# Attention scores in four quadrants, maximum subtracted on GpSimd, transposes and value products two units later

## The chip, the cores and the metric

The kernel runs on one core of a Trainium2 chip. The metric is the device time in microseconds (us) from start to end of one execution. The core has a matrix engine (TensorE, in profiles PE, with its weight loads as PEld), VectorE (DVE), ScalarE (ACT), GpSimd (POOL) and SyncE (SP), which here issues the transfers from main memory (DMA).

## The reference

Three stages follow each other. Sparse attention over 4 batches and 8 heads of 576 positions and head size 64; then a layer that mixes all tokens into 32 slots, passes the slots through eight small expert networks and mixes them back; then a gated feed-forward layer (2304 tokens, 512 to 1536 and back).

```python
scores = scale * np.matmul(q, k.transpose(0, 1, 3, 2))
mask_local = (rel >= 0) & (rel < stride)                  # stride = 32
mask_strided = (rel >= 0) & (pos[None, :] % stride == pos[:, None] % stride)
scores = np.where(masks[None, :, :, :], scores, -1000000000.0)
scores = scores - np.max(scores, axis=-1, keepdims=True)
attn = np.exp(scores)
attn = attn / (np.sum(attn, axis=-1, keepdims=True) + 1e-09)
return np.matmul(attn, v).astype(np.float32)
...
logits = x @ phi
slot_input = d.T @ x                     # d: softmax of logits over tokens
h = np.maximum(slot_input[e] @ w1[e], 0.0); slot_out[e] = h @ w2[e]
return (c @ slot_out)                    # c: softmax of logits over slots
...
return (silu * val @ w_out)              # silu = g * sigmoid(g), g = x @ w_gate, val = x @ w_val
```

## The kernel before

Attention goes in 16 units; a unit is two batches (b = 0, 1) of one head, with queries and keys of batch b on partitions 64b to 64b+63. For the strided heads the positions are permuted, so that every query block of 64 (there are 9, index i) needs a window of 96 keys at most. A unit passes through these steps:

- `qk`: per block and batch one matmul of 64 rows, 64 output partitions and 96 columns, in float32, which takes two instructions each (36 a unit, "sc"). Batch b reads partitions 64b up and writes partitions 64b up. VectorE scales and adds the mask in two pieces of 5 and 4 blocks (480 and 384 columns) and reduces each to the negated maximum `mx`.
- `expo`: nine ScalarE exponentials of 96 columns, with `mx` as bias.
- `tr`: nine transposes by TensorE, and three ScalarE copies into `attile`, one buffer for all units.
- `pv`: 36 instructions of 65 columns (values and a column of ones), then on VectorE the division by the sum into the tile `x`.
- `load_v` brings the next values (64 partitions); GpSimd copies three pieces down to 32 more partitions (L283). Two buffers for values, three for queries and keys.

Every two units, `xtr` (nine transposes of `x`) and `logits` follow; once per pair of batches come `tok_...`, `etr` (transposes of the slot weights) and `slot` (36 instructions, L453). `tok_copy` and `e_perm` are copies of logits and exponentials. The loop over n works on unit n in `qk`/`expo` and on unit n-1 in `tr`/`pv`. All engines run their queues in the order in which the code is written; lists (`at_step`, `at_mid`, `at_first`, `at_late`) put side work into a turn of the loop. Weights of the experts stream in meanwhile: each half tile is 512 KB, `WSCHED` says how many are issued in a turn, from the same SP queue as queries, keys and values. Their homes are 15 buffers of 1 MB and, late, the buffers of attention that come free. `conv` turns packed 64-bit weights into float32 (10 steps a tile, two on ScalarE and eight on VectorE); `PRECONV` and `EXCONV` say how many steps in which turn.

In the feed-forward stage a step n computes gate and value products (`gv`: 2 matmuls, a SiLU on ScalarE, a product on VectorE, a rounded copy `hh` on ScalarE, and the rest `hl` on GpSimd), and three steps later (`LAG`) the output products `omm`; `evac` copies finished sums out of PSUM on VectorE and ScalarE. `room` decides when conversions of later weights are put in.

## Time and profile before

| | us |
|---|---|
| median of three runs (lowest, highest) | 344.02 (342.22, 344.08) |
| the profiled execution | 345.55 |
| its span, first to last instruction | 343.8 |
| TensorE busy in the span | 330.6 |
| VectorE, ScalarE, GpSimd busy | 226.3, 192.8, 121.4 |

The span holds three stretches: attention and slots up to 106.1 us, expert networks up to about 141 us, and feed-forward up to the end. A busy time is an engine's own instructions; the profiled execution has 1.75 us outside its span.

### The profile page before, as it was taken

The numbers are of one execution on the slowest core, as the hardware profiler recorded it, in microseconds if no ns is written. First come the engines' busy times: TensorE is split into PE (matmuls) and PEld (weight loads), VectorE is DVE, ScalarE is ACT, GpSimd is POOL, SyncE is SP. The second block draws the span as 40 slices with busy tenths as digits, with TensorE's granted clock in tenths as the row PEclk, the third lists the DMA queues.
The fourth block names the chain that finished last, engine by engine and source line by source line (L and its number), as shares of the span: only waits on it lengthen the run. The fifth ranks groups of instructions, "written<-read, shape, count | busy, mean of one in ns | idle before, by whom it ended". The sixth has DMA issues, their size and how long they took to land.

```text
span 343.8 us, 7397 instructions
## 1 busy us (share of the span) xinstructions
PE 330.6 (96%) x2857; PEld 248.2 (72%) x2857; DVE 226.3 (66%) x475; ACT 192.8 (56%) x457; POOL 121.4 (35%) x140
## 2 busy tenths in 40 slices
PE   8979999999999999989998999999999999999995
PEld 5868888778775442557785777777878888888894
DVE  6958988998661357477978989899882241424332
ACT  3967899786730123566766576655554343534351
POOL 2133232223200200242353365744577344343441
PEclk9989999999999999998999999999999999999999
DMA  7999999997999999903333544460000030111131
GB/s 277 414 409 375 390 380 378 408 403 248 356 413 400 410 408 408 376 7 124 124 122 126 204 143 139 128 240 1 0 2 0 1 122 3 61 61 62 63 123 61
DMA packets 20803, 71.93 MB, mean 209 GB/s; under 512 B 2336, under 2 KB 2720, under 8 KB 20768
## 3 DMA queue, kind: packets, MB, share of 16 engines
q1 hardware_dynamic: 20624, 71.45, 54.9%
q8 instruction: 22, 0.36, 0.4%
q14 instruction: 13, 0.11, 0.1%
q10 hardware_dynamic: 144, 0.01, 0.0%
HBM read 66.73 MB, written 4.72 MB: 208 GB/s over the span
## 4 chain that ended last, share of the span: by engine, by line
PE 81%; ACT 7%; DVE 5%; DMA 4%; issue 2%; DVEq 0%; SPq 0%; POOL 0%; POOLq 0%
PE o L848 42%; PE pv L742 4%; PE pv L338 4%; PE sc L651 4%; PE sc L305 4%; PE gv L821 4%; PE tr L322 3%; PE gv L822 3%; ACT tmp L315 3%; DMA v<-in_vh 2%; PE tr L357 2%; PE gv L801 2%; DMA k<-in_kq 2%; PE lg L379 1%; PE gv L808 1%
## 5 line engine op out<-in xcount | busy, mean ns | idle before, releaser
L830 POOL TENSOR_TENSOR hl<-h,hh 128x512 fp32r<-128x512 f32 (+1 forms) x60 | 72.5, 1208 | 103.0 <-ACT hh L829 102.9
L848 PE MATMUL o<-woh,hh 128*128 128x512 f32 (+1 forms) x224 | 87.0, 390 | 2.3 <-ACT acc L873 2.2
L848 PE MATMUL o<-wol,hh 128*128 128x512 f32 (+1 forms) x224 | 86.5, 389 | 0.0
L828 DVE TENSOR_TENSOR h<-gv,sg 128x512 f32<-128x512 f32 (+1 forms) x59 | 37.6, 637 | 61.7 <-ACT sg L827 44.1
L848 PE MATMUL o<-woh,hl 128*128 128x512 f32 (+1 forms) x224 | 66.7, 391 | 0.0
L829 ACT CAST hh<-h 128x512 fp32r<-128x512 f32 (+1 forms) x60 | 34.7, 578 | 51.1 <-DVE h L828 51.1
L848 PEld LDWEIGHTS o<-woh,hh 128*128 128x128 f32 x224 | 42.3, 189 | 12.3 <-ACT acc L873 3.0
L848 PEld LDWEIGHTS o<-woh,hl 128*128 128x128 f32 x224 | 42.3, 191 | 9.2
L848 PEld LDWEIGHTS o<-wol,hh 128*128 128x128 f32 x224 | 42.4, 189 | 8.8
L827 ACT ACTIVATE sg<-gv 128x512 f32<-128x512 f32 (+1 forms) x60 | 33.3, 556 | 24.7 <-PE gv L821 22.6
L283 POOL COPY v<-v 32x390 f32<-32x390 f32 (+1 forms) x48 | 22.6, 503 | 63.4 <-DMA v<-in_vh 47.6
L315 ACT ACTIVATE tmp<-tmp,mx 128x96 f32<-128x96 f32 x144 | 40.2, 368 | 8.3 <-DVE mx L310 8.1
L305 PE MATMUL sc<-k 64*64 64x96 f32 x576 | 27.4, 245 | 0.6 <-DMA k<-in_kq 0.5
L305 PEld LDWEIGHTS sc<-k 64*64 64x64 f32 x576 | 24.4, 133 | 3.0 <-issue 1.4
L821 PE MATMUL gv<-cs,St 128*128 128x512 f32 (+1 forms) x60 | 25.6, 426 | 0.0
L338 PEld LDWEIGHTS pv<-v,tmp 96*64 96x64 f32 x576 | 20.0, 140 | 6.3 <-ACT tmp L323 5.7
L792 POOL TENSOR_TENSOR wol<-wo,woh 128x512 fp32r<-128x512 f32 x12 | 15.3, 1301 | 25.5 <-ACT woh L789 25.5
L338 PE MATMUL pv<-v,tmp 96*64 96x65 f32 x576 | 22.3, 229 | 2.0 <-DMA v<-in_vh 1.8
L323 ACT COPY tmp<-tr 96x384 f32<-96x384 f32 x48 | 19.6, 478 | 7.9 <-PE tr L322 7.8
L822 PE MATMUL gv<-cs,St 128*128 128x512 f32 (+1 forms) x59 | 22.3, 378 | 1.1 <-DVE h L828 0.8
L322 PE MATMUL tr<-cst_t,tmp 128*96 128x128 f32 x144 | 21.0, 281 | 1.0 <-ACT eT L443 0.7
L243 DVE SCALAR_TENSOR_TENSOR cv<-g,cv 128x512 int32<-128x512 int32 x30 | 20.8, 692 | 0.7
(165 smaller groups left out, 448.0 us busy)
## 6 DMA issues: line engine op xcount, KB each, us to landing
w<-in_w SPq DMA_DIRECT2D x47, 512.0 KB, 8.5
g<-in_wgv SPq DMA_DIRECT2D x10, 1024.0 KB, 5.0
k<-in_kq SPq DMA_DIRECT2D x16, 576.0 KB, 7.8
g<-in_wo SPq DMA_DIRECT2D x5, 1024.0 KB, 4.9
v<-in_vh SPq DMA_DIRECT2D x16, 292.5 KB, 6.1
wx<-in_w SPq DMA_DIRECT2D x9, 512.0 KB, 6.9
out<-osb SPq DMA_DIRECT2D x17, 256.0 KB, 2.1
w<-in_wgv SPq DMA_DIRECT2D x4, 512.0 KB, 8.8
```

The source lines that it names most:

```text
L283: POOL.tensor_copy(t4[0:W - 64, :, i0:i1, :], t4[64:W, :, i0 - 1:i1 - 1, :])
L305: PE.matmul(out=ps[h, W * (i - i0):W * (i - i0) + W], lhsT=q[h, 64 * i:64 * i + 64], rhs=k[h, c0:c0 + W], start=True, stop=True, skip_grou ...
L315: ACT.activation(out=e[:, i], in_=e[:, i], func=AF.Exp, scale=1.0, bias=mx[:, i:i + 1])
L322: PE.transpose(ps[0:W, 128 * j:128 * j + 128], e[:, 3 * t + j], ident)
L338: PE.matmul(out=ps[64 * b:64 * b + 64, 65 * (i - i0):65 * (i - i0) + 65], lhsT=attile[0:W, i, 64 * b:64 * b + 64], rhs=v[0:W, 65 * (NT * b ...
L821: PE.matmul(out=pg[:, 0:n], lhsT=St[f][:, 0:128], rhs=csf[:, t0:t0 + n], start=True, stop=True)
L822: PE.matmul(out=pvv[:, 0:n], lhsT=St[f][:, 128:256], rhs=csf[:, t0:t0 + n], start=True, stop=True)
L827: ACT.activation(out=sg[:, 0:n], in_=pg[:, 0:n], func=AF.Silu)
L828: DVE.tensor_tensor(out=h[:, 0:n], in0=pvv[:, 0:n], in1=sg[:, 0:n], op=ALU.mult)
L829: ACT.copy(hh[bi, f][:, 0:n], h[:, 0:n])
L830: POOL.tensor_tensor(out=hl[bi, f][:, 0:n], in0=h[:, 0:n], in1=hh[bi, f][:, 0:n].bitcast(F32), op=ALU.subtract)
L848: PE.matmul(out=o[:, 0:c], lhsT=(a, a, l)[i][:, 128 * t:128 * t + 128], rhs=(woh, wol, woh)[i][f][:, c * k:c * k + c], start=(first and i ...
```

## The change

Each unit's 18 score products are spread over all four quadrants of the array: batch b still reads row half b, but even and odd blocks write output halves 0 and 1, and each batch has a PSUM bank of its own. `place(b, i)` says in which slot of the score tile, and on which half of its partitions, a block then stands. A 19th product fills the part of the last slot that a full-width read covers. VectorE adds the masks in three pieces (480 and 384 columns, and 96 on half the partitions). GpSimd adds the negated maximum to the scores, in two pieces; `expo` is two exponentials without bias. `expo` works on unit n-1, `tr` and `pv` on unit n-2, and `tr` is the first thing of a turn. The strided masks are five tiles instead of nine. Copies of `xtr` are all on ScalarE, so are `tok_copy`, and `e_perm` of the first pair. `WSCHED` and `TL` set the turns of weight loads anew, `PRECONV`, `EXCONV`, `ORDER` and `ROOMS` those of conversions. In the feed-forward stage the `hh` and `hl` of the first two steps (`DEFER`) are written one step later.

```diff
-EXCONV = {12: 2, 13: 2, 14: 2, 19: 1, 20: 1, 21: 1, 22: 1}
+EXCONV = {12: 2, 13: 3, 14: 1, 17: 1, 19: 1, 20: 1, 21: 1}
...
-MSC = 6
+MSC = 2
+DEFER = 2
...
+TOKA = (0, 1)
+TOKB = (0,)
...
-XTD = {(1,1,1):(0,1),(1,0,0):(0,1,2)}
+XTD = {}
...
-ROOMS = (0.8, 1.2, 0.6)
+ROOMS = (0.8, 1.2, 0.3)
...
-WSCHED = [2]*12+[2,2,2,2,0]
+WSCHED = [1, 0, 3, 2, 3, 2, 2, 2, 1, 2, 2, 1, 3, 2, 3, 3, 2, 2, 4]
...
+def place(b, i):
+    return (2 * (i // 2) + b, i % 2) if i + 1 < NT else (i, b)
...
-        for i0, i1 in zip(CUT, CUT[1:]):
-            ps = bank("sc", 2)
-            for i in range(i0, i1):
-                c0 = 64 * i
-                for b in range(2):
-                    h = slice(64 * b, 64 * b + 64)
-                    PE.matmul(out=ps[h, W * (i - i0):W * (i - i0) + W], lhsT=q[h, 64 * i:64 * i + 64],
-                              rhs=k[h, c0:c0 + W], start=True, stop=True, skip_group_check=True)
...
+        bk = [bank("sc", 2) for _ in range(2)]
+        last = NT - 1
+        for i, b, c in [(2 * g + d, b, d) for g in range(4) for b, d in ((0, 0), (1, 1), (0, 1), (1, 0))] + \
+                [(last, 0, 0), (last, 1, 1), (last, 0, 1)]:
+            h = slice(64 * b, 64 * b + 64)
+            PE.matmul(out=bk[b][64 * c:64 * c + 64, W * (i // 2):W * (i // 2) + W], lhsT=q[h, 64 * i:64 * i + 64],
+                      rhs=k[h, 64 * i:64 * i + W], start=True, stop=True, skip_group_check=True)
...
+        for o, p, m in ((e[:, 0:9:2], p5[0], m5), (e[:, 1:8:2], p5[1][:, 0:4], m5[:, 0:4]),
+                        (e[64:128, last], p5[1][64:128, 4], m5[64:128, 4])):
+            DVE.scalar_tensor_tensor(out=o, in0=p, scalar=0.125, in1=m, op0=ALU.mult, op1=ALU.add)
+        for s0, s1 in zip(CUT, CUT[1:]):
+            DVE.tensor_reduce(out=mx[:, s0:s1], in_=e[:, s0:s1], axis=AX, op=ALU.max, negate=True)
+            POOL.tensor_tensor(out=e[:, s0:s1], in0=e[:, s0:s1],
+                               in1=mx[:, s0:s1].unsqueeze(2).to_broadcast([128, s1 - s0, W]), op=ALU.add)
...
-        for i in range(CUT[k], CUT[k + 1]):
-            ACT.activation(out=e[:, i], in_=e[:, i], func=AF.Exp, scale=1.0, bias=mx[:, i:i + 1])
+        a = etile(u)[:, CUT[k]:CUT[k + 1]]
+        ACT.activation(out=a, in_=a, func=AF.Exp)
...
-        while n < 16 or any(k >= n for k in late):
...
+        while n < 18 or any(k >= n for k in late):
+            if 2 <= n < 18:
+                tr(n - 2)
             if n < 16:
                 qk(n)
                 load_qk(n + NQK)
             if 0 <= n - 1 < 16:
-                tr(n - 1)
...
+                expo(n - 1, 0)
...
+            if 2 <= n < 18:
+                pv(n - 2)
+                load_v(n)
...
             ACT.activation(out=sg[:, 0:w], in_=pg[:, 0:w], func=AF.Silu)
+            while late_hh:
+                late_hh.pop(0)()
...
+            if n < DEFER:
+                late_hh.append(split)
+            else:
+                split()
```

Two turns of TensorE's queue in the middle of attention, before ("sc" are the scores, "tr" over `tmp` the transposes of a unit, "tr" over `x` those of `xtr`, "lg" the logits, `k_76` to `k_78` the three buffers of queries and keys, `v_79` and `v_80` those of values):

```order
L305 MATMUL sc<-k_76 64x96 x18
L322 MATMUL tr<-cst_t,tmp 96x128 x9
L379 MATMUL lg<-xT,phi_t 32x16x18 x4
L338 MATMUL pv<-v_80,tmp 64x65 x18
L305 MATMUL sc<-k_77 64x96 x18
L322 MATMUL tr<-cst_t,tmp 96x128 x9
L338 MATMUL pv<-v_79,tmp 64x65 x18
L357 MATMUL tr<-cst_t,x 128x128 x9
```

The same place of TensorE's queue after the change, also two turns:

```order
L337 MATMUL tr<-cst_t,tmp 96x128 x9
L316 MATMUL sc<-k_77 64x96 x19
L395 MATMUL lg<-xT,phi_t 32x16x18 x4
L354 MATMUL pv<-v_80,tmp 64x65 x18
L337 MATMUL tr<-cst_t,tmp 96x128 x9
L316 MATMUL sc<-k_78 64x96 x19
L354 MATMUL pv<-v_79,tmp 64x65 x18
L373 MATMUL tr<-cst_t,x 128x128 x9
```

The transposes moved ahead of the scores, so that the scores now stand between every `tr` and its `pv`.

GpSimd's queue at the start of the loop, before (`v0` and `v1` are the two buffers of values, each copied in three pieces):

```order
L283 COPY v0_79<-v0_79 32x2x130
L283 COPY v0_79<-v0_79 32x2x195 x2
L283 COPY v1_80<-v1_80 32x2x130
L283 COPY v1_80<-v1_80 32x2x195 x2
L283 COPY v0_79<-v0_79 32x2x130
```

The same stretch of GpSimd's queue after the change (`mx_134`, `mx_167`, `mx_225`, `mx_306` are the maxima of units 0 to 3):

```order
L295 COPY v0_79<-v0_79 32x2x130
L295 COPY v0_79<-v0_79 32x2x195 x2
L295 COPY v1_80<-v1_80 32x2x130
L295 COPY v1_80<-v1_80 32x2x195 x2
L325 TENSOR_TENSOR tmp_83<-tmp_83,mx_134 128x480
L325 TENSOR_TENSOR tmp_83<-tmp_83,mx_134 128x384
...
L325 TENSOR_TENSOR tmp_83<-tmp_83,mx_225 128x480
L325 TENSOR_TENSOR tmp_83<-tmp_83,mx_225 128x384
L295 COPY v0_79<-v0_79 32x2x130
L295 COPY v0_79<-v0_79 32x2x195 x2
L325 TENSOR_TENSOR tmp_83<-tmp_83,mx_306 128x480
```

The additions of a unit now stand behind the value copies of the unit before it.

ScalarE's queue at the start of the feed-forward stage, before (`sg` is the SiLU, `hh` the rounded copy, `wg` a conversion step, `acc` an evacuation):

```order
L827 ACTIVATE sg<-gv 128x512
L829 CAST hh<-h 128x512
L827 ACTIVATE sg<-gv 128x512
L829 CAST hh<-h 128x512
L221 ACTIVATE wg_2157<-g 128x512 x2
L827 ACTIVATE sg<-gv 128x512
L829 CAST hh<-h 128x512
```

The same place of ScalarE's queue after the change:

```order
L838 ACTIVATE sg<-gv 128x512 x2
L844 CAST hh<-h 128x512
L233 ACTIVATE wg_2106<-g 128x512 x2
L838 ACTIVATE sg<-gv 128x512
L844 CAST hh<-h 128x512 x2
```

The first two copies `hh` moved one step down, behind the next step's SiLU.

## Rows read from the trace of the kernel before

**Rows 1.** The page: busy us (share of the span) xinstructions of three engines

```profile
PE 330.6 (96%) x2857; PEld 248.2 (72%) x2857; DVE 226.3 (66%) x475; ACT 192.8 (56%) x457; POOL 121.4 (35%) x140
```

**Rows 2.** Windows: span; PE, PEld, DVE, ACT, POOL busy; clock; DMA share, GB/s

```profile
20.00:30.00 10.00, 9.87 (x162) 8.34 (x160) 5.49 (x16) 6.08 (x20) 3.28 (x9) 0.83 1.02 409
40.00:50.00 10.00, 10.00 (x185) 8.46 (x183) 8.33 (x22) 9.03 (x30) 3.19 (x7) 1.00 1.01 386
50.00:60.00 10.00, 10.00 (x189) 8.63 (x187) 8.56 (x23) 9.08 (x29) 3.21 (x8) 1.00 1.01 382
150.00:160.00 10.00, 8.34 (x28) 6.14 (x28) 6.66 (x11) 5.95 (x11) 3.32 (x4) 0.83 0.33 107
```

**Rows 3.** The chain that ended last, two units: start us, us, what

```profile
39.10 1.77 PE sc L305 x36
40.87 1.12 PE tr L322 x9
...
43.33 1.13 PE tr L357 x9
...
47.25 0.62 PE lg L379 x8
47.88 1.20 PE pv L338 x36
49.08 1.63 PE sc L305 x36
```

**Rows 4.** The same chain, landmarks of attention

```profile
11.26 8.40 DMA v<-in_vh
...
22.26 2.08 PE tr L357 x9
...
75.04 2.15 PE tr L453 x36
...
91.53 2.36 PE tr L357 x18
...
106.10 13.44 PE sc L651 x119
```

**Rows 5.** Groups by line and shape: busy us, mean ns, idle before

```profile
L315 ACT ACTIVATE tmp<-tmp,mx 128x96 f32<-128x96 f32 x144 | 40.2, 368 | 8.3 <-DVE mx L310 8.1
L309 DVE SCALAR_TENSOR_TENSOR tmp<-sc,mt 128x480 f32<-128x480 f32 x16 | 10.4, 651 | 1.6 <-PE sc L305 1.1 <-ACT wg L221 0.3
L309 DVE SCALAR_TENSOR_TENSOR tmp<-sc,mt 128x384 f32<-128x384 f32 x16 | 8.8, 548 | 0.0
L698 ACT ACTIVATE cf<-cf 96x384 f32<-96x384 f32 x2 | 1.0, 522 | 2.5 <-DVE cf L696 2.5
L830 POOL TENSOR_TENSOR hl<-h,hh 128x512 fp32r<-128x512 f32 x26 | 33.7, 1296 | 52.3 <-ACT hh L829 52.3
L830 POOL TENSOR_TENSOR hl<-h,hh 128x256 fp32r<-128x256 f32 x4 | 3.0, 738 | 3.9 <-ACT hh L829 3.9
L438 PE MATMUL tr<-cst_t,e 128*64 128x128 f32 x16 | 1.8, 298 | 0.0
L434 PE MATMUL tr<-cst_t,e 128*128 128x128 f32 x16 | 2.4, 283 | 0.0
```

**Rows 6.** Timeline: value copies on GpSimd, a conversion on VectorE; issues of values

```profile
59.61 1.30 POOL L283 COPY v<-v 32x260 f32<-32x260 f32 x3 [3.26 <-DMA v<-in_vh]
72.65 2.23 POOL L283 COPY v<-v 32x260 f32<-32x260 f32 x3 [7.04 <-DMA v<-in_vh]
72.69 1.82 DVE L243 SCALAR_TENSOR_TENSOR wg<-w,wg 128x512 int32<-128x512 int32 x2
v<-in_vh SPq DMA_DIRECT2D x16, 292.5 KB, 6.1
```

**Rows 7.** Start of feed-forward: timeline of TensorE's wait, then the chain

```profile
152.85 0.50 PE L848 MATMUL o<-woh,hh 128*128 128x512 f32 x1 [1.42 <-ACT acc L873]
152.85 4.61 PE o L848 x12
157.92 2.75 PE o L848 x12
```

More of the change, by code (lines that the diff above doesn't have):

```diff
@@ L99, in constants @@
     c[:, 3], c[:, 4], c[:, 5], c[:, 15] = q, q + 32, q + 16, np.maximum(q, 31)
-    for i in range(NT):
-        c[:, 6 + i] = (64 * i + q) // 18 * 18 - 64 * i + 32
+    for g in range(5):
+        i = np.minimum(2 * g + p // 64, NT - 1)
+        c[:, 6 + g] = (64 * i + q) // 18 * 18 - 64 * i + 32
     return c
@@ L337, in pv @@
                 for b in range(2):
-                    PE.matmul(out=ps[64 * b:64 * b + 64, 65 * (i - i0):65 * (i - i0) + 65], lhsT=attile[0:W, i, 64 * b:64 * b + 64],
+                    s, c = place(b, i)
+                    PE.matmul(out=ps[64 * b:64 * b + 64, 65 * (i - i0):65 * (i - i0) + 65], lhsT=attile[0:W, s, 64 * c:64 * c + 64],
                               rhs=v[0:W, 65 * (NT * b + i):65 * (NT * b + i) + 65], start=True, stop=True, skip_group_check=True)
@@ L405, in e_perm @@
         for hf in hfs:
-            DVE.tensor_copy(e2[bp][64:128, 288 * hf:288 * hf + 288].rearrange("p (r t) -> p r t", t=18),
+            (ACT.copy if bp in TOKB else DVE.tensor_copy)(e2[bp][64:128, 288 * hf:288 * hf + 288].rearrange("p (r t) -> p r t", t=18),
                             e2[bp][0:64].rearrange("p (t r) -> p r t", r=32)[:, 16 * hf:16 * hf + 16])
@@ L417, in tok_copy @@
         for hf in range(2):
-            DVE.tensor_copy(Lb[r].rearrange("p (t r) -> p t r", r=32)[:, :, 16 * hf:16 * hf + 16],
+            (ACT.copy if bp in TOKA else DVE.tensor_copy)(Lb[r].rearrange("p (t r) -> p t r", r=32)[:, :, 16 * hf:16 * hf + 16],
                             lg[bp][64 * hf:64 * hf + 64, 0:288].rearrange("p (t r) -> p t r", r=16))
@@ L440, in etr @@
         p4 = ps[:, 0:128 * (z - a)].rearrange("p (j y b s) -> p j y b s", y=2, b=2, s=32)
-        for b, cp_ in ((0, ACT.copy), (1, ACT.copy)):
+        for b, cp_ in ((0, ACT.copy), (1, DVE.tensor_copy if (bp, g) in ETD else ACT.copy)):
             w0, w1 = (max(a, 1), z) if b == 0 else (a, min(z, NT))
@@ L815, in build, with gv @@
         csf = cs.rearrange("p a b -> p (a b)")
-        def gv(bi, f):
-            t0, n = BLOCKS[bi]
+        late_hh = []
+        def gv(n, bi, f):
+            t0, w = BLOCKS[bi]
             n0 = start.pop(0) if start else 2
             pg, pvv = [bank("gv", 3) if k < n0 else bank("o", 4) for k in range(2)]
-            PE.matmul(out=pg[:, 0:n], lhsT=St[f][:, 0:128], rhs=csf[:, t0:t0 + n], start=True, stop=True)
-            PE.matmul(out=pvv[:, 0:n], lhsT=St[f][:, 128:256], rhs=csf[:, t0:t0 + n], start=True, stop=True)
+            PE.matmul(out=pg[:, 0:w], lhsT=St[f][:, 0:128], rhs=csf[:, t0:t0 + w], start=True, stop=True)
+            PE.matmul(out=pvv[:, 0:w], lhsT=St[f][:, 128:256], rhs=csf[:, t0:t0 + w], start=True, stop=True)
             sg = fl.tile([128, 512], F32, tag="sg", name="sg", bufs=2)
@@ L826, in gv, with split @@
             hl[bi, f] = fl.tile([128, 512], F32R, tag="hl", name="hl", bufs=LAG + 1)
-            ACT.activation(out=sg[:, 0:n], in_=pg[:, 0:n], func=AF.Silu)
-            DVE.tensor_tensor(out=h[:, 0:n], in0=pvv[:, 0:n], in1=sg[:, 0:n], op=ALU.mult)
-            ACT.copy(hh[bi, f][:, 0:n], h[:, 0:n])
-            POOL.tensor_tensor(out=hl[bi, f][:, 0:n], in0=h[:, 0:n], in1=hh[bi, f][:, 0:n].bitcast(F32),
-                               op=ALU.subtract)
+            ACT.activation(out=sg[:, 0:w], in_=pg[:, 0:w], func=AF.Silu)
+            while late_hh:
+                late_hh.pop(0)()
+            DVE.tensor_tensor(out=h[:, 0:w], in0=pvv[:, 0:w], in1=sg[:, 0:w], op=ALU.mult)
+            def split(a=hh[bi, f], b=hl[bi, f]):
+                ACT.copy(a[:, 0:w], h[:, 0:w])
+                POOL.tensor_tensor(out=b[:, 0:w], in0=h[:, 0:w], in1=a[:, 0:w].bitcast(F32), op=ALU.subtract)
+            if n < DEFER:
+                late_hh.append(split)
+            else:
+                split()
         ob = {}
@@ L996, in build @@
                 room -= part(n)
-            if n >= STG:
+            m = n + 1 - LAG
+            if n >= STG and not (n in NOSTG or (AVOID and 0 <= m < len(seq) and seq[m][2] == CUTS[seq[m][1]][seq[m][0] + 1] - 1)):
                 stage(n)
```

65 lines of the change are left out of this document (27 added, 38 removed).

## Prediction

> **What bounds the kernel now.** I read the page first: TensorE is busy for 96% of the span [rows 1], so time is won only where TensorE gets less to do or where its work is stretched. The windows say where to look: from 40 to 60 us TensorE is busy all the time, while VectorE (8.3 to 8.6 us of 10), ScalarE (9.0 to 9.1) and DMA (share 1.01, 382 to 386 GB/s) are nearly full too [rows 2]. The chain of waits is a plain TensorE chain there: two units take 49.08 - 39.10 = 9.98 us, 4.99 a unit, made of scores 1.63, transposes 1.12, value products 1.20, and every second unit 1.13 for the transposes of x and 0.62 for logits [rows 3]. The landmarks bound the stretch that the change touches: the value products of unit 2 end at 22.26, those of unit 15 at 91.53, and the experts' weights begin at 106.10, 14.57 us later [rows 4]. So 13 units take 69.3 us. TensorE's own work in them is 13 x (1.63 + 1.12 + 1.20) + 6 x (1.13 + 0.62) + slot transposes (1.8 + 2.4)/2 = 2.1 [rows 5] + slot sums 2.15 [rows 4] = 66.1 us; the other 3.2 are waits and a stretch from 20 to 30 us with a granted clock of 0.83 [rows 2], that is, part of it at 1.2 instead of 2.4 GHz, after TensorE had waited for values (the 8.40 us from the issue of a transfer to its landing, [rows 4]).
>
> **The scores.** 36 instructions take 1.63 us, 45 ns each, on two quadrants [rows 3]. There will be 38 on four. Bounds: no faster, 38 x 45 ns = 1.72 us; twice as fast, 38 x 22.6 = 0.86. The nearest row is the value product, 33 ns an instruction with 65 columns [rows 3], so 0.51 ns a column against the scores' 0.47: neither shows a floor, both go with columns. I take 28 ns, 1.05 us, in the middle between the 33 of that row and 22.6. That takes 0.58 us off each unit's path.
> Beside this, the Trainium skill (TensorE: Matmul & The Clock Gate, in the section Wait — 56ns, not 53.3ns?) says that the distance from one matmul's start to the next does not go below about 25 ns however few columns it has. By that the scores would take 38 x 25 ns = 0.95 us, an estimate from that page, and TensorE's floor below would be 80.5 instead of the 81.6 of my 1.05 us; a full doubling to 0.86 would be out of reach. The densest small product shown here, 33 ns, does not contradict it.
>
> **ScalarE** gives nine exponentials (40.2 us for 144, 0.28 each, 2.5 a unit [rows 5]) for two of 480 and 384 columns. The exponential of 96x384 takes 0.52 [rows 5], so about 0.52 + 0.60 = 1.1. It takes over copies of 0.5 each, one to two a unit at most. ScalarE falls from 9 us of 10 to about 7 and hides.
>
> **VectorE** gets a third mask piece of 96 columns: by 0.651 for 480 and 0.548 for 384 [rows 5], 0.24 us; the moved copies take about as much off. It stays at (8.33 + 8.56)/2 per 10 us x 0.499 = 4.2 us a unit.
>
> **GpSimd** gets two additions. Its subtractions of 128x512 and 128x256 take 1.296 and 0.738 [rows 5], so 480 columns take 1.23 and 384 take 1.02. With 1.30 for the value copies [rows 6] that is 3.55 us a unit, under any of the turns below. They are queued behind the copies, which wait for a transfer: who waits for the addition is the exponential, and for that the transposes. The loop to check is: value products of unit n-2 end, values n land 6.1 us after their issue [rows 6], copies 1.30, additions of n+1 1.23 + 1.02, second exponential 0.52, the last transposes 0.4, scores 1.05, logits 0.3 on average, value products n+1 1.20: 13.1 us in three turns, 4.37 a unit.
>
> **Where attention then ends.** At the start the first additions stand behind both first value copies, which delays unit 0, while fewer weights are ahead of the third values. I let the value products of unit 2 end at 24, 1.7 us later than before (22 to 26). From there four floors hold to the end of unit 15:
> TensorE, with two score sets already done: 24 + 11 x 1.05 + 13 x (1.12 + 1.20) + 7 x 1.13 + 6 x 0.62 + 2.1 + 2.15 = 81.6.
> DMA: before the last values the queue holds 16 x 0.59 MB of queries and keys, 16 x 0.30 of values and, by the new table, 32 half tiles of 0.524: 31.1 MB. At the 409 GB/s of rows 2 this is 76 us, from 1.2 on, then copies 1.3 and product 1.2: 79.7, and up to 2 us later if the queue runs dry in the first turns.
> VectorE: 24 + 13 x 4.2 = 78.6, without pauses.
> The loop over GpSimd: 24 + 13 x 4.37 = 80.8.
> They lie within 3 us, so each one's jitter becomes another's wait. Before, with TensorE's floor well above the rest, 3.2 us were lost; I take 4.1 above the highest floor, 85.7. The gain is 91.53 - 85.7 = 5.8 us. It costs nothing behind it: the 14.57 us up to the experts hold the same steps, and the last weights hang on buffers that attention frees, so they move with it.
>
> **The feed-forward start.** TensorE waits 1.42 us for ScalarE's evacuation, which stands behind a rounded copy that waits for VectorE; then the clock falls, and twelve products take 4.61 us where the next twelve take 2.75 [rows 7], in the window with a granted clock of 0.83 [rows 2]. With the copies moved one step down, ScalarE runs the second SiLU while VectorE makes the first product, and the third copy is done earlier. At most 1.42 + 1.86 = 3.3 us are won, at least none, since conversions on VectorE bind again soon after. I take half, 1.6. The new places of conversion steps and the order of loads I cost at nothing: they are as many as before and lie beside TensorE work.
>
> **The sum** against the profiled execution: 345.55 - 5.8 - 1.6 = 338.1. That execution is 1.53 above the median 344.02, so the time is **336.6**.
>
> **Rivals.**
> First, GpSimd becomes the bound, and the kernel gets slower. Evidence for: three value copies took 2.23 us instead of 1.30 just while VectorE ran two conversion steps for 1.82 us [rows 6], 1.72 times as long; additions are GpSimd work that reads the same memory. If all of GpSimd's 3.55 us were stretched so, a unit would take 6.1 us: 13 x 6.1 = 79.3 instead of 69.3, and with the feed-forward gain 344.0 + 10 + 1.7 - 1.6 = 354. It decides from a stretch of 1.41 on (3.55 x 1.41 = 4.99). Against: only some 16 conversion steps fall into 16 units.
> The Trainium skill (SBUF — State Buffer, in the section SBUF: two separate sides) says that VectorE and GpSimd share a port pair that one locks for a whole instruction, for VectorE steps with two inputs there or in a two-port mode. The pair of rows 6 agrees with that. By it the masks and maxima, which read scores from PSUM or have one input, would not collide, and this rival would not come.
> Second, values come late. If the landing takes 8 us instead of 6.1 because the queue is always full, the loop over GpSimd takes 15 us, 5.0 a unit, as now, and only the waits at the start and in the middle go: attention gains 2, feed-forward 1, 341.
> Third, four quadrants are no faster than two: 1.72 for the scores makes TensorE's floor 81.6 + 11 x 0.67 = 89.0, attention ends at about 90, gain 1.5, and with 1 of feed-forward 341.5.
> Fourth, everything goes well: TensorE's floor is reached (gain 9.9) and the clock does not fall (3.3): 344.0 - 13.2 = 331.
>
> **Chances.** The forecast (334 to 340) 0.50, the fourth 0.15, the second 0.17, the third 0.08, the first 0.08, others 0.02. The range leaves out the first rival and the outermost ends of the fourth and second: 331 to 343. One per cent, 3.4 us, is about what a measurement of this kernel can tell from no change. Faster by more (below 340.6): the forecast, the fourth and half of second and third, 0.78; within it 0.14; slower 0.08.
>
> **What would show it.** The score group should fall from 1.63 us to 0.9 to 1.25; at 1.6 the third rival holds. The exponentials should take 1.1 us a unit, the additions 2.25; at 3.5 or more with TensorE's waits ending in GpSimd, the first. The value products of unit 15 should end at 83 to 88, the first expert product start 14 to 15 us later. If the transposes wait for exponentials, these for additions, and these for value copies that wait for DMA, it is the second. In feed-forward the wait for the evacuation should be shorter and the granted clock in that stretch nearer 1.00. What would make me wrong most easily is the friction of 4.1 us, which no row prices, and the start, where a long idle time of TensorE could lower its clock.

## The result, and the profile after

The changed kernel takes 345.24 us (343.36 to 346.93, nine runs) where the kernel before, run beside it, takes 342.74 (342.22 to 344.08, nine runs): ratio 1.006 [1.0031, 1.0088]. A second comparison on another chip gives 344.69 against 344.13, 1.0004 [0.9976, 1.0033]. One run of again_after and one of quad below were in a slower state of the chip; every ratio goes by the other runs and is not the quotient of the medians beside it. So the change is worth nothing, or costs up to 0.9%; 336.6 was forecast, and the range ended at 343.

The page, busy time by engine. TensorE is busy 10.9 us less than before [rows 1], GpSimd 28 more:

```profile
PE 319.7 (94%) x2889; PEld 237.5 (70%) x2889; DVE 227.2 (67%) x477; ACT 176.1 (52%) x356; POOL 149.6 (44%) x172
```

The windows [rows 2], with the one from 30 to 40 us added. TensorE is not full any more in three of the four windows of attention (in the other its clock is 0.87); the transfers (last two columns: share and GB/s) and VectorE (third busy time) are, in three of four. The granted clock of 0.83 that stood in the feed-forward stage is not seen here:

```profile
20.00:30.00 10.00, 8.95 (x198) 7.23 (x196) 9.68 (x25) 5.49 (x13) 5.88 (x10) 1.00 1.00 386
30.00:40.00 10.00, 6.90 (x120) 5.60 (x116) 9.74 (x20) 4.50 (x11) 5.65 (x9) 0.96 1.02 410
40.00:50.00 10.00, 10.00 (x188) 8.15 (x186) 7.98 (x21) 7.38 (x17) 7.56 (x13) 0.87 0.91 322
50.00:60.00 10.00, 8.79 (x186) 6.91 (x184) 9.57 (x27) 5.90 (x15) 5.93 (x10) 1.00 1.00 369
150.00:160.00 10.00, 10.00 (x50) 7.55 (x49) 8.88 (x15) 7.72 (x16) 5.57 (x5) 1.00 0.30 103
```

The chain that ended last, two units in the middle [rows 3]. The scores are 0.98 us instead of 1.63, but a chain of TensorE alone holds only for a stretch:

```profile
47.92 1.13 PE tr L373 x9
49.06 1.21 PE tr L337 x9
50.27 0.98 PE sc L316 x38
51.25 0.62 PE lg L395 x8
...
60.16 1.01 PE sc L316 x38
61.27 1.14 DVE tmp L322 x2
62.71 1.11 DVE mx L324 x2
64.38 0.82 DVE x L361 x2
66.55 1.04 DVE wg L251 x2
```

From 61 to 82 us it runs through VectorE: masks, maxima, divisions and conversion steps of several units in a row. The start of the same chain [rows 4]: value transfer, both value copies, addition, exponential, and only then the first transposes, which take 2.16 us at half clock where 1.12 is usual.

```profile
1.63 5.04 DMA v<-in_vh
6.73 1.30 POOL v L295 x3
...
8.93 1.31 POOL v L295 x3
10.32 1.00 POOL tmp L325
11.34 0.61 ACT tmp L330
11.99 2.16 PE tr L337 x9
```

The groups that answer to [rows 5] (busy us, mean ns, idle before). Exponentials and the third mask piece are as priced, additions cheaper:

```profile
L330 ACT ACTIVATE tmp<-tmp 128x480 f32<-128x480 f32 x16 | 9.7, 607 | 21.3 <-POOL tmp L325 21.2
L330 ACT ACTIVATE tmp<-tmp 128x384 f32<-128x384 f32 x16 | 8.4, 523 | 3.6 <-POOL tmp L325 3.5
L325 POOL TENSOR_TENSOR tmp<-tmp,mx 128x480 f32<-128x480 f32 x16 | 16.1, 1007 | 5.9 <-PE tr L337 4.3 <-DVE mx L324 0.4 <-ACT xT L375 0.2
L325 POOL TENSOR_TENSOR tmp<-tmp,mx 128x384 f32<-128x384 f32 x16 | 14.7, 916 | 0.0
L322 DVE SCALAR_TENSOR_TENSOR tmp<-sc,mt 64x96 f32<-64x96 f32 x16 | 4.2, 261 | 0.5
L259 DVE SCALAR_TENSOR_TENSOR wg<-w,wg 128x512 int32<-128x512 int32 x4 | 3.9, 987 | 0.0
L237 DVE TENSOR_SCALAR wg<-wg 128x512 f32<-128x512 f32 x4 | 3.6, 938 | 0.0
```

The chain at the start of the feed-forward stage [rows 7]. The second dozen of output products follows the first without a wait or a fall of the clock:

```profile
149.10 3.03 PE o L867 x12
...
152.60 2.75 PE o L867 x12
```

**The landmarks** tell where the time went. I read four from each profile: the end of the value products of unit 2, the time from there to those of unit 15, the first expert product, and the time from the end of the last second-layer expert product to the end of the 37th instruction of the output products ("ff start"). All times in us; ratio and interval are to the kernel before run beside it (its medians there lie between 342.74 and 344.13), so compare ratios and not medians across rows.

| kernel | unit 2 ends | 2 to 15 | experts at | ff start | median time | ratio, interval |
|---|---|---|---|---|---|---|
| before | 22.3 | 69.3 | 106.0 | 22.1 | 342.74 | 1 |
| again_before | 21.2 | 68.9 | 104.6 | 20.5 | 342.82 | one run |
| changed | 24.7 | 68.5 | 107.7 | 18.4 | 345.24 | 1.006 [1.0031, 1.0088] |
| again_after | 25.6 | 68.0 | 108.2 | 18.4 | 344.69 | 1.0004 [0.9976, 1.0033] |
| no_add | 26.1 | 65.1 | 105.7 | 18.4 | 344.21 | 1.0023 [0.9992, 1.0053] |
| no_conv | 24.9 | 69.2 | 108.7 | 18.3 | 344.73 | 1.0008 [0.9975, 1.004] |
| late_copy | 27.8 | 68.6 | 110.9 | 18.3 | 346.54 | 1.0079 [1.0064, 1.0094] |
| nv3 | 28.2 | 65.0 | 107.8 | 19.3 | 347.03 | 1.0091 [1.0066, 1.0116] |
| act_bias | 27.6 | 69.3 | 111.4 | 18.3 | 346.31 | 1.0068 [1.0039, 1.0098] |
| ff_only | 21.1 | 68.9 | 104.5 | 18.3 | 340.6 | 0.9912 [0.9888, 0.9937] |
| quad | 21.2 | 69.5 | 105.2 | 18.5 | 343.35 | 0.9996 [0.9961, 1.0032] |
| lag2 | 28.0 | 68.0 | 110.6 | 18.4 | 348.41 | 1.0133 [1.0084, 1.0181] |
| light | 25.5 | 65.2 | 105.3 | 18.5 | 356.62 | 1.0392 [1.0348, 1.0436] |
| lean | 28.2 | 61.2 | 103.9 | 18.4 | 354.21 | 1.0313 [1.0281, 1.0345] |
| early_w | 25.7 | 69.7 | 110.0 | 18.3 | 343.97 | 1.0021 [0.9998, 1.0044] |
| early_both | 24.6 | 67.1 | 106.3 | 18.4 | 343.45 | 1.0007 [0.9983, 1.0031] |
| quad_w | 21.5 | 73.7 | 109.7 | 18.6 | 344.94 | 1.0067 [1.0036, 1.0097] |
| ff_only_w | 21.6 | 68.7 | 104.9 | 18.3 | 340.88 | 0.9914 [0.9885, 0.9943] |
| early_warm | 26.0 | 65.2 | 105.7 | 18.3 | 343.21 | 0.9987 [0.9966, 1.0007] |

The changed kernel wins 2.1 us at the feed-forward start (3.7 against the first profile of before, where the clock fell there). It loses 3 us in attention, all at the start: unit 2 ends 3.5 us later than in again_before, the second profile of the kernel before. And from unit 2 to unit 15, where 12 sets of scores of 1.63 us are now 11 of 0.98, 8.8 us less for TensorE, it wins less than one. TensorE's work did shrink. Here are 65 us of attention (columns as in the windows) of again_before, then of the changed kernel:

```profile
25.00:90.00 65.00, 63.24 (x1119) 52.35 (x1118) 53.86 (x136) 53.22 (x170) 20.05 (x39) 1.00 0.97 373
```

```profile
25.00:90.00 65.00, 56.87 (x1116) 45.73 (x1115) 58.08 (x147) 41.55 (x95) 39.60 (x62) 0.97 0.96 358
```

TensorE's idle time rose from 1.8 to 8.1 us. So two questions: what fills the 8 us, and what delays the start.

### The profile page after: what moved, and what is told of

It reads as the page before. It is cut to its first block, busy times and chain, and to the rows that moved or that the text cites. A ratio compares the mean times of both kernels' runs of the same rounds, so it can differ in the third digit from the quotient of the medians.

```text
span 341.6 us, 7400 instructions
## 1 busy us (share of the span) xinstructions
PE 319.7 (94%) x2889; PEld 237.5 (70%) x2889; DVE 227.2 (67%) x477; ACT 176.1 (52%) x356; POOL 149.6 (44%) x172
## 4 chain that ended last, share of the span: by engine, by line
PE 78%; DVE 12%; issue 3%; ACT 2%; POOL 2%; DMA 1%; SPq 0%; DVEq 0%; POOLq 0%; ACTq 0%
PE o L867 42%; PE pv L751 4%; PE sc L660 4%; PE gv L832 4%; PE gv L833 3%; PE tr L337 3%; DVE tmp L322 3%; PE sc L316 3%; PE pv L354 3%; DVE mx L324 2%; PE gv L810 2%; DMA v<-in_vh 1%; DVE x L361 1%; PE tr L373 1%; PE gv L817 1%
## 5 line engine op out<-in xcount | busy, mean ns | idle before, releaser
L867 PE MATMUL o<-woh,hl 128*128 128x512 f32 (+1 forms) x224 | 65.9, 387 | 0.0
L867 PEld LDWEIGHTS o<-woh,hl 128*128 128x128 f32 x224 | 41.7, 188 | 9.0
L295 POOL COPY v<-v 32x390 f32<-32x390 f32 (+1 forms) x48 | 20.8, 465 | 32.9 <-DMA v<-in_vh 16.6
L325 POOL TENSOR_TENSOR tmp<-tmp,mx 128x480 f32<-128x480 f32 (+1 forms) x32 | 30.1, 962 | 5.9 <-PE tr L337 4.3
L330 ACT ACTIVATE tmp<-tmp 128x480 f32<-128x480 f32 (+1 forms) x32 | 17.8, 565 | 24.9 <-POOL tmp L325 24.7
L337 PE MATMUL tr<-cst_t,tmp 128*96 128x128 f32 x144 | 21.6, 297 | 7.0 <-ACT tmp L330 3.5
L322 DVE SCALAR_TENSOR_TENSOR tmp<-sc,mt 128x480 f32<-128x480 f32 (+2 forms) x48 | 22.0, 485 | 6.8 <-PE sc L316 4.7
L801 POOL TENSOR_TENSOR wol<-wo,woh 128x512 fp32r<-128x512 f32 x12 | 15.3, 1297 | 25.5 <-ACT woh L798 25.5
L832 PE MATMUL gv<-cs,St 128*128 128x512 f32 (+1 forms) x60 | 25.6, 426 | 0.0
L354 PEld LDWEIGHTS pv<-v,tmp 96*64 96x64 f32 x576 | 18.7, 137 | 8.1 <-issue 3.5
L354 PE MATMUL pv<-v,tmp 96*64 96x65 f32 x576 | 20.7, 224 | 2.8 <-issue 1.2
L337 PEld LDWEIGHTS tr<-cst_t,tmp 128*96 128x96 f32 x144 | 15.7, 133 | 10.5 <-ACT xT L375 4.5
```

The costliest lines, as they stand in the source:

```text
L295: POOL.tensor_copy(t4[0:W - 64, :, i0:i1, :], t4[64:W, :, i0 - 1:i1 - 1, :])
L322: DVE.scalar_tensor_tensor(out=o, in0=p, scalar=0.125, in1=m, op0=ALU.mult, op1=ALU.add)
L325: POOL.tensor_tensor(out=e[:, s0:s1], in0=e[:, s0:s1], in1=mx[:, s0:s1].unsqueeze(2).to_broadcast([128, s1 - s0, W]), op=ALU.add)
L337: PE.transpose(ps[0:W, 128 * j:128 * j + 128], e[:, 3 * t + j], ident)
L354: PE.matmul(out=ps[64 * b:64 * b + 64, 65 * (i - i0):65 * (i - i0) + 65], lhsT=attile[0:W, s, 64 * c:64 * c + 64], rhs=v[0:W, 65 * (NT * b ...
L832: PE.matmul(out=pg[:, 0:w], lhsT=St[f][:, 0:128], rhs=csf[:, t0:t0 + w], start=True, stop=True)
```

## The experiments

Each expectation names its theories, and their letters change from batch to batch. In the first, A is that VectorE is full and the additions stretch its work, B that the additions are a link in the loop from values to value products; in the second, A is the queue on GpSimd, B the two value buffers and C the bytes of all transfers.

**Both kernels again, and one load at a time.** again_before and again_after are the kernels unchanged.

> The kernel before, unchanged, for a second profile. Its first profiled execution took 345.55 us, above all nine timed runs (342.22 to 344.08). If the clock that fell at 153 us there (twelve products in 4.61 us instead of 2.75) is a chance of that execution, this profile shows 2.75 to 3 there and a span of 340 to 342; if it belongs to the kernel, 4.6 again and 343 to 344.

> The changed kernel, unchanged, for a second profile and more timed runs. Both theories (VectorE full and stretched, or the loop over values and additions) expect the value products of unit 15 to end at 92 to 95 us again, and 1.003 to 1.009 of the time before.

The second profile of before shows no fall of the clock anywhere in its span; the 4.61 us of [rows 7] were a chance of that execution. Against it the feed-forward gain is 2.1 us. again_after ends unit 15 at 93.6 us, as expected, but its ratio of 1.0004 lies under the 1.003 to 1.009 expected.

no_add leaves the additions out; no_conv leaves out VectorE's steps of the conversions that run during attention:

```diff
-            POOL.tensor_tensor(out=e[:, s0:s1], in0=e[:, s0:s1],
-                               in1=mx[:, s0:s1].unsqueeze(2).to_broadcast([128, s1 - s0, W]), op=ALU.add)
...
             _, fn, k = q.pop(0)
-            fn(k)
+            if fn.__name__ == "mag":
+                fn(k)
```

> The changed kernel without the two GpSimd additions of a unit: the maximum is still reduced but not subtracted (left out). Theory A, VectorE is the full engine in attention and GpSimd's additions stretch its conversion steps: the steps of conversion go back from about 0.95 us to 0.7, units are no longer held, value products of unit 15 end at 85 to 88, 5 to 7 us off the time. Theory B, the additions matter as a link of the loop (values land, copies, additions, exponentials): the same gain or more, 6 to 9 us, with conversion steps as long as before. If neither holds, under 2 us.

> The changed kernel without VectorE's steps of the 30 early conversion steps (of the first three packed weight tiles only the first ScalarE step is left; what they hold is not the weight). Theory A: VectorE loses 16 steps of about 0.95 us in attention, so units of 20 to 80 us shorten and the value products of unit 15 end 6 to 9 us earlier, at 84 to 87. Theory B: the additions and landings are untouched, at most 2 us.

no_add missed both theories: without additions the units shorten by 3 us, but unit 2 ends later still, at 26.1. no_conv misses A and fits B (at most 2 us), against which no_add speaks: nothing shortens, although VectorE's busy time in the 65 us falls from 58.1 to 46.5. Neither load alone is the bound.

**The value path.** late_copy moves the value copies of a unit behind the next unit's additions; nv3 has a third value buffer, earlier transfers, and copies behind the unit's own additions; act_bias subtracts the maximum as before. (`shift_v` holds the three copies, split off `load_v`.)

```diff
 # late_copy
             if 0 <= n - 1 < 16:
+                shift_v(n - 1)
                 expo(n - 1, 0)
 # nv3
-NB = 15
-NV = 2
+NB = 14
+NV = 3
...
+                shift_v(n)
...
-                load_v(n)
+            if 1 <= n < 15:
+                load_v(n + 1)
 # act_bias: no POOL.tensor_tensor, and in expo
+        for i in range(CUT[k], CUT[k + 1]):
+            ACT.activation(out=e[:, i], in_=e[:, i], func=AF.Exp, scale=1.0, bias=mx[:, i:i + 1])
```

> The changed kernel, except that GpSimd's three value copies of a unit stand one unit later in its queue, behind the next unit's additions instead of ahead of them, so no addition waits for a transfer of values. Theory A (the gain is lost because the additions, and with them the exponentials and TensorE, queue on GpSimd behind copies that wait 5 to 6 us for a transfer): the second and third unit start without the wait of 3.5 us at 12 us, value products of unit 2 end at 21 to 22.5 (24.7 and 25.6 in the two profiles of the changed kernel), units 2 to 15 take 65 to 66 us (68.0 and 68.5), and the time is 5 to 6 us less than the changed kernel's: 338 to 340, ratio to before 0.982 to 0.990. Theory B (the two value buffers: the next transfer starts only when the value products of two units before have ended, lands 5.5 us later and is copied in 1.3): the start gains its 2 to 3 us, units 2 to 15 still take 68, 341 to 342. Theory C (the bytes of all transfers up to unit 15 set its end): the start's gain is given back, unit 15 ends at 93, 343 to 345.

> The changed kernel with three value buffers instead of two and one expert-weight buffer less (two halves of a weight are loaded later for it), the transfer of a unit's values issued one unit earlier, and the value copies behind the unit's own additions. Theory B (two value buffers): values have landed before their copies are due, GpSimd waits for a values' transfer less than 5 us in all up to unit 15 (20 to 30 us before), units 2 to 15 take 62 to 65 us, unit 15 ends at 84 to 88, and the time is 335 to 339. Theory A (queue on GpSimd alone): the same as with the copies moved alone, within 1 us. Theory C (bytes): unit 15 ends at 92 to 94, 343 to 345.

> The changed kernel, with the maximum subtracted as before by nine exponentials of a unit on ScalarE (its bias), and no additions on GpSimd. Theory A (queue on GpSimd): units 2 to 15 take 65 to 67 us, the exponentials' 2.5 us of ScalarE for a unit find room beside 4.5 of a unit, value products of unit 2 end at 22 to 24, and the time is 340 to 342, ratio 0.988 to 0.995. Theories B and C (two value buffers, or bytes): units 2 to 15 take 68 to 69 us as with the additions, 343 to 345.

No theory held for late_copy: it is slower, and GpSimd now waits 18.8 us for maxima and TensorE 5.5 us for value copies. With nv3 the waits for values are gone (GpSimd has none of 0.9 us or more in sum from 15 to 92 us) and the units take 65.0, as B says, but unit 2 ends at 28.2, and the experts, one weight buffer short, take 3 us longer. act_bias brings the old 69.3 back. In all three the start got worse, whatever became of the additions.

**The parts by themselves.** ff_only is the kernel before with `DEFER`, `ROOMS` and the order of the weights 8 and 10; quad adds the four quadrants to it (the matmuls, `place` and the masks of the section on the change) and nothing else: units one step apart, nine exponentials, old tables; lag2 is the changed kernel with the old scores and exponentials: distance and tables alone.

```diff
 # ff_only, quad
-ROOMS = (0.8, 1.2, 0.6)
+ROOMS = (0.8, 1.2, 0.3)
+DEFER = 2
 # lag2, in act_bias
-    return (2 * (i // 2) + b, i % 2) if i + 1 < NT else (i, b)
+    return i, b
...
+        for i0, i1 in zip(CUT, CUT[1:]):
+            ps = bank("sc", 2)
```

> The kernel before with nothing but the three changes at the feed-forward start (two of gate and value kept back, the order of the weights 8 and 10, the third limit 0.3). All theories: attention stays as before, unit 15 ends at 90 to 92 and the experts start at 104.5 to 106; from the end of the second expert products to the end of the 24th output product it takes 18.4 us, where the kernel before took 20.5 in the profile without a fall of TensorE's clock there. So the time is 1.8 to 2.4 us under the kernel before beside it, ratio 0.993 to 0.995. If it is as slow as before, the gain at the feed-forward start hangs on the changed attention.

> The kernel before with the feed-forward start changed and the scores in quadrants (with the masks and places of blocks that go with them), and nothing else: transposes and value products one unit later as before, nine exponentials with the maximum as bias, no additions on GpSimd, all tables as before. Theory S (the quadrants are worth what was expected; the loss comes from the two units' distance, which leaves TensorE empty at the start): value products of unit 2 end at 20 to 22 as before, units 2 to 15 take 61 to 65 us instead of 69, unit 15 ends at 83 to 87, the time is 334 to 337. Theory L (a unit is held up by VectorE, transfers and the loops between engines as much as by TensorE, so shorter scores turn into waits of TensorE): unit 2 as before, units 2 to 15 take 67 to 69 us, TensorE's busy share falls from 9.5 to 9.9 of 10 to about 9, the time is 339 to 341, as with the feed-forward start alone.

> The changed kernel with the scores as before (36 matmuls of 128 rows' halves in two parts), the maximum as the bias of nine exponentials and no additions on GpSimd: the two units' distance, the tables of the early weights and the feed-forward start remain. Theory S (the distance empties TensorE at the start): value products of unit 2 end at 25 to 28, TensorE's clock falls to half somewhere between 8 and 22, units 2 to 15 take 68 to 70 us, and the time is 344 to 348, 4 to 7 us over the kernel with the feed-forward start alone. The rival (the start is lost to the additions or the quadrants): unit 2 ends at 20 to 22 and the time is 339 to 342.

ff_only gives more than expected, 0.9912 [0.9888, 0.9937]: 2.2 us in the profiles, and 3.2 in the medians. It is the fastest version here. quad answers Theory L in kind (units 67 to 69 us), though not in its time of 339 to 341. The quadrants take TensorE's busy time of the 65 us to 56.85, as in the changed kernel, and the units take 69.5 as without them:

```profile
25.00:90.00 65.00, 56.85 (x1124) 44.76 (x1125) 54.78 (x146) 53.13 (x170) 18.52 (x39) 1.00 0.96 370
```

Its chain that ended last shows what holds them: from 38.51 to 49.10 it runs through VectorE, ScalarE, TensorE and VectorE again, and TensorE has 3.1 of these 10.6 us, in which two units pass.

```profile
38.51 1.04 DVE tmp L316 x2
...
39.86 0.67 DVE mx L318
...
40.55 2.50 ACT tmp L323 x9
43.05 0.55 ACT wg L227
43.61 0.37 ACT xT L368
...
44.02 1.28 PE tr L330 x9
45.30 0.62 PE lg L388 x8
45.92 1.23 PE pv L347 x36
...
47.62 0.82 DVE x L354 x2
48.44 0.66 DVE wg L231
49.10 1.04 DVE tmp L316 x2
```

lag2 answers for the start: with neither quadrants nor additions, distance and tables end unit 2 at 28.0 and cost 2.2% against ff_only. Its trace shows one cause on ScalarE: the absolute value of an early weight (L232) waits for a transfer that the new `WSCHED` and `PRECONV` put late, and the copies of the first transposes (L334) stand behind it. The bracket is the engine's idle time before the instruction and what ended it:

```profile
16.03 0.66 ACT L232 ACTIVATE wg<-w 128x512 f32<-128x512 f32 x1 [4.19 <-DMA w<-in_wgv]
16.59 1.22 ACT L334 COPY tmp<-tr 96x384 f32<-96x384 f32 x3
```

Its first value products begin at 17.15 behind it, TensorE having stood still for 5.50 us, and the clock is at half from 14.0 to 20.8 us.

**Transfers, and the loads together.** light moves 12 halves of weights behind the last values; lean does so and also leaves out the additions and the conversion steps, as above.

```diff
-WSCHED = [1, 0, 3, 2, 3, 2, 2, 2, 1, 2, 2, 1, 3, 2, 3, 3, 2, 2, 4]
+WSCHED = [1, 0, 3, 1, 1, 1, 1, 1, 1, 1, 1, 1, 1, 2, 2, 2, 6, 6, 8]
```

> The changed kernel with 12 of the 32 halves of expert weights that are loaded ahead of the last values moved behind them (WSCHED 1, 0, 3, then ten times 1, three times 2, then 6, 6, 8), 6.3 MB or 15 us of transfers. Only the landmarks of attention are to be read; the experts may start short of weights. Theory D (transfers set attention's pace): values land in 3 to 4 us instead of 5.5, units 2 to 15 take 61 to 64 us instead of 68. Theory L (several limits near each other, none alone): units 2 to 15 take 65 to 68 us, and the time does not fall under 341. The start up to unit 2 stays at 24 to 26 by either.

> The changed kernel with three loads taken away together: GpSimd's additions (the maximum is not subtracted), VectorE's steps of the early conversions (these weights are left unconverted), and the 12 halves of weights moved behind the last values. Alone the first two left the time where it was. Theory L (several limits stand near each other, and where one is taken away the next holds the same unit up): together they let TensorE run nearly without waits, units 2 to 15 take 60 to 63 us (its own work there is 59 to 60), unit 15 ends at 84 to 88. If a limit is left that none of the three touches (the loops between the engines with their fixed order): 64 us or more, and TensorE's busy share stays under 9.3 of 10.

This is Theory L again, in numbers: with the 12 halves moved 65.2, without additions 65.1, without conversion steps 69.2, and with all three 61.2, against 68.0 and 68.5. So moving transfers and dropping additions are worth some 3 us each, and the three together 7. In lean TensorE is busy 61.2 of the 65 us from 25 to 90, with the transfers' share at 0.87. (Both kernels are slow in the end because the experts then wait for their weights.)

**The start, one wait after the other.** early_w issues both halves of the first weight at the start; early_both also puts the additions of units 0 and 1 ahead of the first value copies; early_warm adds 12 matmuls on zeros there.

```diff
-WSCHED = [1, 0, 3, 2, 3,
+WSCHED = [2, 0, 2, 2, 3,
 # early_both
+            if n == 1:
+                shift_v(0)
+                shift_v(1)
 # early_warm
+            if n < 3:
+                warm((4, 6, 2)[n])
```

> The changed kernel with one number moved in the table of early weights: both halves of the first weight are issued at the start (2, 0, 2, 2 in place of 1, 0, 3, 2), as in the kernel before, so that ScalarE's second absolute value of the early conversion finds its data instead of waiting 1.3 to 4.3 us with the transposed copies queued behind it. Theory W (two waits stand one behind the other at the start: the additions behind the value copies, then the absolute value behind its transfer; either alone gives little): the first wait (3.5 to 4 us at 12 us) stays, the second goes, value products of unit 2 end at 22.5 to 24.5 (24.7 and 25.6), and the time is 0 to 2 us less than the changed kernel's. If the second wait costs nothing: unit 2 at 24.7 to 25.6 as before it.

> The changed kernel with both waits at the start taken away: the two halves of the first weight issued at the start, and on GpSimd the additions of units 0 and 1 ahead of the value copies of units 0 and 1; all later units as in the changed kernel. Theory W: TensorE doesn't stand still at 8 to 12 and 14 to 16 us, its clock does not fall there, value products of unit 2 end at 20.5 to 22.5, and 3 to 4 us of the time go: 340.5 to 342.5 where the changed kernel took 343.4 to 345.2. The rival (the two units' distance itself costs the start): unit 2 still at 24 to 28, time 343 to 345.

> The kernel with both waits at the start taken away (early_both), with 12 matmuls on a tile of zeros put between the first scores and transposes (four behind the scores of unit 0, six behind those of unit 1, two behind those of unit 2), so that TensorE does not stand empty there. Theory K (what is left of the late start is TensorE's clock, which fell to half from 11.6 to 18.4 us because TensorE was busy 6.3 of the first 10 us with shorter scores): the clock stays full up to 20 us, value products of unit 2 end at 20.5 to 22.5 instead of 24.6, the time falls by 2 to 3 us to 340.5 to 341.5. The rival (the two units' distance makes the start long at full clock too): the clock stays, unit 2 still ends at 23.5 to 25, the time stays at 343 to 344.

early_w loses the second wait and wins nothing at the start: unit 2 ends at 25.7, not at the 22.5 to 24.5 of Theory W, since TensorE still waits 4.79 us for the first. early_both shortens the first: TensorE's longest wait before 13 us is 1.42 us, for 3.54 in the changed kernel; ScalarE still waits 0.80 and 0.61 us for the early weight (1.31 there). The time is 343.45 after 345.24 and 344.69, which the intervals hardly separate; unit 2 ends at 24.6 and the clock still fell, so Theory W missed and its rival's numbers came. early_warm keeps the clock full until 25.8 us, and unit 2 ends at 26.0; the last of its 36 instructions came 1.6 us behind the others, which end at 24.1. Theory K, 20.5 to 22.5, fell; its rival's range, 23.5 to 25, holds for those 35 instructions and not for the landmark. What in the distance costs the time is not shown. VectorE (third busy time below) is full there from 10 to 30 us. With the clock kept and the first wait shortened, the changed kernel is level with before (0.9987 [0.9966, 1.0007]), and 0.75% behind ff_only.

```profile
10.00:20.00 10.00, 8.11 (x166) 6.30 (x168) 9.71 (x24) 6.26 (x13) 6.20 (x11) 1.00 1.02 402
20.00:30.00 10.00, 7.92 (x128) 7.06 (x127) 9.68 (x24) 4.85 (x11) 6.66 (x10) 0.83 1.00 388
```

**Is it the transfers in quad?** quad_w and ff_only_w move five halves from units 2 to 10 to units 12 to 15.

```diff
-WSCHED = [2]*12+[2,2,2,2,0]
+WSCHED = [2, 2, 2, 1, 2, 1, 2, 1, 2, 1, 2, 1, 2, 3, 3, 4, 1]
```

> The kernel with the scores in quadrants and the changed feed-forward start, with five halves of weights moved from units 2 to 10 to units 12 to 15, where the transfers' share is 0.8. Theory D (in units 2 to 10 of this kernel every second unit waits for its values, which land 7 to 7.7 us after the value products that free their buffer, behind 3.9 MB that a pair of units transfers): values land in 5 to 6.5 us, units 2 to 10 take 35 to 37 us instead of 39.4, unit 15 ends at 87 to 89 and the time falls by 2 to 3 us. If the engines' own order holds the units and not the transfers: units 2 to 10 take 39 us as before.

> The kernel before with the changed feed-forward start and the same five halves of weights moved from units 2 to 10 to units 12 to 15; the scores stay as they were. Theory D with a TensorE that is full at 9.5 to 10 of 10: units 2 to 10 take 39 to 40 us as without the move (40.3), the time is 340 to 341.5. If units 2 to 10 shorten here as much as with the quadrants (35 to 37 us), TensorE was not a bound at all in the kernel before, and the transfers alone were.

Theory D missed in quad_w: values land in 4.9 us instead of 6.5 (medians), and units 2 to 10 take 41.7 us instead of 39.4, with a fall of the clock from 46.4 to 49.8 us. At half clock 3.4 us can cost at most 1.7, which leaves 40.0, above the forecast of 35 to 37. So in quad the order of the engines holds the units, as its chain above shows, and not these transfers. ff_only_w went as expected: 40.1 us, and the same time. With the old scores TensorE is full, whatever the transfers do.

## Why the prediction was wrong, point by point

**The prices of the parts were right.** Scores 0.98 us for 1.05 forecast; exponentials 0.61 + 0.52 for 1.1; the third mask piece 0.26 for 0.24; additions 1.01 + 0.92 for 1.23 + 1.02. Beside the first: the estimate from the 25 ns that the Trainium skill gives (TensorE: Matmul & The Clock Gate, in the section Wait — 56ns, not 53.3ns?) was 0.95; the trace agrees, with 26 ns each.

**The step that failed is "Where attention then ends": "I take 4.1 above the highest floor".** Four floors within 3 us were set up, and one friction was put on top. Measured, units 2 to 15 took 68.0 and 68.5 us where TensorE's floor from 24 was 57.6, so 10 to 11 us of waits in place of 4.1. lean, with three loads lightened, has 61.2 - 57.6 = 3.6. So TensorE's floor and a friction near 4 fit lean, in which other limits are further off, and not a kernel in which VectorE, the transfers, GpSimd and the chain through the engines stand near it. quad shows that this needs neither GpSimd nor the distance: the quadrants alone give nothing.

**Two steps under it failed too: the path, and "That takes 0.58 us off each unit's path".** "The chain of waits is a plain TensorE chain there" is true of the 10 us of [rows 3]. Over all 69.3 us from unit 2 to unit 15 the same chain has 43.0 us on TensorE, 14.4 on ScalarE and 10.6 on VectorE; in quad it has 26.8, 21.9 and 19.3. A little ahead of [rows 3] it runs so:

```profile
31.73 0.57 DVE tmp L309
32.39 0.67 DVE mx L310
33.08 2.50 ACT tmp L315 x9
```

And the shorter scores bring the exponentials no nearer. Here is, of units 3 to 15, one in which the first exponential follows soonest on the start of the scores, from the timelines of again_before and then quad:

```profile
47.53 1.70 PE L305 MATMUL sc<-k 64*64 64x96 f32 x36
...
49.25 0.64 DVE L309 SCALAR_TENSOR_TENSOR tmp<-sc,mt 128x480 f32<-128x480 f32 x1
...
50.85 2.51 ACT L315 ACTIVATE tmp<-tmp,mx 128x96 f32<-128x96 f32 x9
```

```profile
22.23 1.05 PE L310 MATMUL sc<-k 64*64 64x96 f32 x38
...
23.34 1.42 DVE L316 SCALAR_TENSOR_TENSOR tmp<-sc,mt 128x480 f32<-128x480 f32 x3 [0.18 <-PE sc L310]
...
25.62 2.51 ACT L323 ACTIVATE tmp<-tmp,mx 128x96 f32<-128x96 f32 x9
```

That is 3.32 us before and 3.39 with the quadrants: all three masks (1.42) now stand ahead of the first maximum, where one (0.64) stood. From the first score to the last value product a unit takes at least 7.65 us in again_before and 7.75 in quad. No run has the quadrants with the maximum of the first blocks ahead of the other masks, so how much of quad's lost gain that order explains is open.

Beside quad: the Trainium skill (TensorEngine Tiling (Array Packing), in the section PSUM Bottleneck) says that tiling speeds up TensorE but not the emptying of PSUM, which may become the bottleneck then. The trace agrees in part: masks (1.04 us for two) and divisions (0.82), which read the products from PSUM, are steps of quad's chain above, but so are the exponentials (2.50) and the maxima (0.67), which do not.

**Two of the floors were mis-sized.** VectorE's 4.2 us a unit came from the windows 40 to 60 us. Over 25 to 90 us again_before has 53.86 us of VectorE in 65, which at 68.9 / 13 = 5.30 a unit is 4.39, and the changed kernel 58.08, which at 5.27 is 4.71. From 24.7 that floor is at 24.7 + 13 x 4.71 = 86, and TensorE's at 82.3. Part of the increase is the conversion steps, which GpSimd stretches (below). It is not the only bound, as no_conv shows. The transfers' floor of 79.7 took 409 GB/s, the fastest window of [rows 2]; at the 382 to 386 of the two others, 31.1 MB take 81 us, and that floor is at 84 to 85. The changed kernel moved 358 GB/s from 25 to 90 us, with a share of 0.96.

**The start was mis-sized too.** "I let the value products of unit 2 end at 24": they ended at 24.7 and 25.6, inside the bounds of 22 to 26. But the second profile of the kernel before, with no fall of the clock, ends them at 21.2, so the loss is 3.5 to 4.4 and not 1.7; 1.0 of it is one more set of scores that is done by then. I named the wait of additions behind value copies, and costed the new tables at nothing: "they are as many as before and lie beside TensorE work". lag2 shows the second wait that they make, and early_w that it hides behind the first.

**The baseline.** The sum was made against 345.55, an execution with the clock at half in two places. What was feared, the start "where a long idle time of TensorE could lower its clock", came true: TensorE, now with gaps, has half clock from 11.9 to 15.4 and 39.2 to 42.7 us in its profile.

**The feed-forward start was right in kind**: 1.6 forecast within 0 to 3.3, 2.1 measured in the profiles, and behind attention nothing was lost, 14.5 us up to the experts as before. Term by term it was not: again_before has the same wait of 1.42 us for the evacuation and no fall of the clock, so the 1.86 of the clock was not there to win, and the wait went whole. That half of both came near is luck.

**The rivals.** The second, values late (341), and the third (341.5) are nearest in time. The second is right in its result, that units stay as long as before, but not by its reason: values land in 5.5 us, not 8. The first did not come: GpSimd is busy 39.6 of 65 us, and its additions stay under their price in the mean. The third did not: the quadrants are faster.

**What stays open**: what part of the late start is the distance and what part VectorE, which is full from 10 to 30 us in early_warm; a kernel with distance one and additions on GpSimd was not tried. Also how much of quad's slower median, 343.35 against 340.6 while the profiles differ by 1.0 us, is the clock: its timed runs have a mean granted clock of 0.975 to 0.999, those of ff_only 0.994 to 1.000. The three runs of quad at 0.995 and more took 340.68 to 341.67, the others, at 0.989 and less, 342.41 to 345.87.

## What to carry to other kernels

An engine that is busy 97% of a stretch (63.24 of 65 us here) is not thereby the only bound: before pricing a cut on it, follow the chain over the whole stretch (not in one good window), sum every other engine's time over it, and add up the chain of one unit through all engines. Here VectorE, 15% below TensorE, the transfers, at a share of 0.97, and that chain took the gain. Friction over one floor says little of friction over four. Take a bundle of changes apart: here the small one at the feed-forward start was worth 0.9%, and the large one in attention took it back.
